# k and q of both head halves ahead of v in a segment-recurrent attention kernel

## The chip, the cores and the metric

One core of one Trainium2 chip. The metric is the device time of one execution in microseconds (us), the median of several. In the profiles PE is the tensor engine, DVE the vector engine, ACT the scalar engine, POOL GpSimd, SP the engine whose queue asks for the weights.

## The reference, cut to what matters

```python
for s in range(64):                       # 2048 tokens in segments of 32
    h = concat([mem, x[32*s:32*s+32]])    # 8 + 32 = 40 rows of 1024
    q, k, v = h @ Wq, h @ Wk, h @ Wv      # 32 heads of 128 each
    p = softmax(where(mask, q @ k.T * scale, -1e9))
    o = (p @ v) @ Wo
    mem = o[:8]                           # the next segment needs this
    outs.append(o[8:])
# then: g * a + (1 - g) * b with b = gelu(x @ w_gate) * (x @ w_up) @ w_down
```

The 64 segments form a chain through mem. Everything else (the feed-forward branch b) has no such chain.

## The kernel before

Each segment is done in two halves of 16 heads (r = 0, 1). The weights of q, k, v and o come in 64 pieces of 512 KB (matrix, half, eighth). They don't all fit into the on-chip memory, so 12 slots are shared by the same eighth of the two halves: after the piece of half 0 has been used, the slot is fetched again for half 1. The next segment takes the halves in the other order, so that one fetch per shared slot and segment is enough.

```python
PAIRS = {"k": (0, 2), "q": (0,), "v": (0, 1, 2, 3, 4, 6), "o": (0, 2, 4)}   # eighths that share a slot
def seq(m, r):        # shared pieces first in half 0, last in half 1
    ...
    return p + f if r == 0 else f + p
walk = both(0) + one("v", 0) + both(1) + one("o", 0) + one("v", 1) + one("o", 1)   # both = k and q
...
def spent(k):         # after the last use of piece k
    n = home[k]
    done[n] += 1
    if done[n] < len(uses[n]) and uses[n][done[n]] != k:
        fetch(n)      # SP asks for the other half's piece
```

Work is hung into this walk of 64 projection steps with `on(matrix, half, step, function)`. "Evac" copies a finished projection out of PSUM, the memory that PE writes; "turning" is transposing by PE; "scores" is q times k, "attend" is the softmax result times v; a_bf is the output of a segment in bf16. The parts that matter:

```python
on("v", 0, 0, lambda: evac(bank_of["k", 0], tok))     # PSUM -> SBUF
on("v", 0, 0, lambda: evac(bank_of["q", 0], tok2))
on("v", 0, 4, lambda: trans(kT, tok))                 # 4 PE transposes, copy to kT
on("v", 0, 7, lambda: trans(qT, tok2))
on("k", 1, 0, lambda: evac(bank_of["v", 0], vA))
on("k", 1, 2, lambda: scores(0))                      # then softmax on DVE and ACT
...
on("o", 0, 0, some(f1, 4))                            # fill: 4 groups of other matmuls
on("o", 0, 0, lambda: trans(kT, tok))
on("o", 0, 0, lambda: attend(ua))
...
on("o", 0, 1, lambda: scores(1, ...))
# end of a segment: PSUM -> a_bf on ACT, two 128-column transposes of a_bf, two DVE copies
# into hT (the mem rows of the next segment); the store of a_bf waits until on("k", 0, 4)
```

"Fills" f1 and f2 are matmuls for the x rows of later segments. In two of every four segments they produce rows of k and q, which are then stored to qk_scr. Every store belongs to a semaphore lane; a transfer in a lane is issued only when the one before it in that lane has landed.

Of the kernel before, what the change touches and what calls it, by code (L numbers as in the profile page):

```python
# [195 lines left out]
def bass_gated_mix__memory_aug_recurrent_mem_tr__geglu_ffn__prompt_kernel(  # L196
# [35 lines left out]
    with ExitStack() as es:  # L232
# [58 lines left out]
        qT = al("qT", [128, 4, 4, 32])  # L291
        cur[0] += 128
# [6 lines left out]
        vA = al("vA", [128, 4, 128], at=oT.off)  # L299
        tok2 = al("tok2", [128, 512], at=oT.off + 1024)  # L300
        tA = al("tA", [128, 8, 32], at=qT.off)
        tB = al("tB", [128, 8, 32], at=qT.off + 512)
        E8 = al("E8", [128, 8, LQ], at=qT.off + 512)
# [14 lines left out]
        PAIRS = {"k": (0, 2), "q": (0,), "v": (0, 1, 2, 3, 4, 6), "o": (0, 2, 4)}  # L318
# [8 lines left out]
        walk = both(0) + one("v", 0) + both(1) + one("o", 0) + one("v", 1) + one("o", 1)  # L327
# [226 lines left out]
        inits = [k for k in [at_step(p, 0) for p in range(24)] + [(m, 1, i) for m in "kqv" for i in range(8)]  # L554
# [129 lines left out]
        def evac(bank, t):  # L684
            act_copy(t[:, :], PB[bank][:, :], [BK(bank)], [t.r()])

        def trans4(e, t=tok, head=False):
            for j in range(4):
                to = PBV[TT][:, 0:512].rearrange("p (g j y) -> p j g y", g=4, j=4)[:, j] if head else PBV[TT][:, j * 128:(j + 1) * 128]
                ins = e.transpose(to, t[:, j * 128:(j + 1) * 128], ident[:, :])  # L690
            return ins

        def trans_pe(t):
            op("pe", lambda e: trans4(e, t), rd=[t.r(), ident.r()], wr=[BK(TT)])

        def trans(to, t):
            if t:
                trans_pe(t)
            i_ap = PBV[TT][:, 0:512].rearrange("p (j g c) -> p (j g) c", g=4, c=32)
            dve_copy(to[:, :, :, 0:32].rearrange("p j g c -> p (j g) c"), i_ap, [BK(TT)], [to.r()])  # L700
# [5 lines left out]
        def scores(r, mid=None):  # L706
# [18 lines left out]
            op("dve", lambda e: e.tensor_tensor(out=sS, in0=sS, in1=b8(nm, LQ), op=ALU.add), rd=[BK(SS), st8.r(0, 8)], wr=[BK(SS)])  # L725
            op("act", lambda e: e.activation(E8[:, :, :].rearrange("p a c -> p (a c)"), PB[SS][:, 0:320], ACTF.Exp, scale=scale),  # L726
               rd=[BK(SS)], wr=[E8.r()])
            if mid:
                mid()
# [14 lines left out]
        bo = (B0, B1, B2, SS)  # L744

        def attend(u):

            def f(e):
                for j in range(4):
                    for g in range(4):  # L750
                        r = slice(32 * g, 32 * g + 32)
                        ins = e.matmul(PB[bo[g]][:, j * OW:(j + 1) * OW], lhsT=vA[r, j, :],
                                       rhs=tA[r, 2 * j:2 * j + 2, :].rearrange("p a c -> p (a c)"),
                                       start=(j == 0), stop=False, skip_group_check=True)
                return ins
            op("pe", f, rd=[vA.r(), tA.r()], wr=[BK(b) for b in bo])

        def attend_tail(u):
# [9 lines left out]
            for g in range(4):  # L768
                cp[("act", "dve")[g % 2]](oT[:, g, :, :].rearrange("p j c -> p (j c)"), PB[bo[g]][:, 0:n], [BK(bo[g])],
                                          [oT.r(g * n, (g + 1) * n)])  # L770
# [5 lines left out]
        bank_of = {("k", 0): B0, ("q", 0): B1, ("v", 0): B2, ("k", 1): B0, ("q", 1): F2, ("v", 1): B0}  # L776
# [37 lines left out]
        def fill(m, u, b, h=hR):  # L814
            ks = [(m, u, i) for i in range(8) if i not in PAIRS[m]] + [(m, u, i) for i in PAIRS[m]]
            out = []
            for n, k in enumerate(ks):
# [7 lines left out]
                out.append(lambda f=f, w=w: op("pe", f, rd=[h.r(), w.r()], wr=[BK(b)]))  # L825
# [23 lines left out]
        def fill_evac(m, u, b, st):  # L849
            t = st if m == "v" else tok  # L850
            act_copy(t[:, :], PB[b][:, :], [BK(b)], [t.r()])

        def fill_trans(m):
            op("pe", lambda e: trans4(e, tok, m == "q"), rd=[tok.r(), ident.r()], wr=[BK(TT)])

        def fill_put(st, how):
            cp[how](st[:, :].rearrange("p (i x c) -> p x i c", i=4, x=16), PBV[TT][:, 0:512].rearrange("p (x i c) -> p x i c", x=16, i=4),
                    [BK(TT)], [st.r()])
# [36 lines left out]
        for s in range(NSEG):  # L895
# [23 lines left out]
            on("k", 0, 4, some(pend))  # L919
            if s == 0:  # L920
# [15 lines left out]
                on("v", 0, 4, lambda: rest_k(0))  # L936

                def fills_1():
# [4 lines left out]
                    act_copy(tok[:, :], PB[F2][:, :], [BK(F2)], [tok.r()])  # L943
                    mm0("v", 1, F1, st1[1])
                    tr0("q", 1, tok, st1[2])
                on("k", 1, 0, fills_1)
                if NG > 1:
                    on("k", 1, 0, lambda: op("dve", lambda e: e.tensor_copy(hR[:, :, :], hR1[:, :, :]), rd=[hR1.r()], wr=[hR.r()]))
                on("k", 1, 0, lambda: (load_v(0, slice(1, 2)), more_late(99)))
                on("q", 1, 0, lambda: load_h(1))  # L950
            if s > 0:
                on("k", 0, 6, lambda: rest_k(0))
            on("v", 0, 0, lambda: evac(bank_of["k", 0], tok))
            on("v", 0, 0, lambda: evac(bank_of["q", 0], tok2))
            on("v", 0, 4, lambda: trans(kT, tok))
            on("v", 0, 7, lambda: trans(qT, tok2))
            on("k", 1, 0, lambda: evac(bank_of["v", 0], vA))
            on("k", 1, 2, lambda: scores(0))
            on("k", 1, 4, lambda: rest_k(1))

# [4 lines left out]
            on("o", 0, 0, lambda: evac(bank_of["k", 1], tok))  # L965
            on("o", 0, 0, lambda: evac(bank_of["q", 1], tok2))
            on("o", 0, 0, some(f1, 4))
            on("o", 0, 0, lambda: trans(kT, tok))
            on("o", 0, 0, some(f1, 2))
            on("o", 0, 0, lambda: trans_pe(tok2))  # L970
            on("o", 0, 0, lambda: attend(ua))
            on("o", 0, 0, lambda: attend_tail(ua))
            on("o", 0, 0, lambda: trans(qT, None))
            on("o", 0, 0, some(f1))
            if k1:
                on("o", 0, 1, lambda: fill_evac(*k1, F1, stage))
            if uw == 1:
                on("o", 0, 1, lambda: act_copy(part[:, :], PB[F1][:, 0:256], [BK(F1)], [part.r()]))
            on("o", 0, 1, lambda: scores(1, add_part if uw == 0 else None))
            if k1:  # L980
                on("o", 0, 6, lambda: fill_trans(k1[0]))
                on("o", 0, 6, lambda: fill_put(stage, "act"))
                on("o", 0, 6, lambda: fill_store(*k1, G, stage))
            if uw == 0:
                on("o", 0, 6, lambda: store_tail(Q, asum))
            on("o", 1, 0, lambda: evac(bank_of["v", 1], vA))
            on("o", 1, 0, some(f2, 6))
            on("o", 1, 0, lambda: attend(ub))
            on("o", 1, 0, lambda: attend_tail(ub))
            on("o", 1, 0, some(f2))  # L990
            if s % 4 == 0 and Q >= 0:
                on("o", 1, 0, lambda: load_oR(Q, 1))
            if s % 4 == 1 and Q >= 0:
                on("o", 1, 0, lambda: load_oR(Q, 0))
            if not last:
                on("o", 1, 0, lambda: load_qk(s + 1, 0))
                on("o", 1, 0, lambda: load_qk(s + 1, 1))
                on("o", 1, 0, lambda: load_v(s + 1))
                if s + 2 < NSEG:
                    on("o", 1, 0, lambda: load_h(s + 2))  # L1000
            if s % 4 == 2 and G + 1 < NG:
                on("o", 1, 0, lambda: load_r(G + 1))
            if k2:
                on("o", 1, 1, lambda: fill_evac(*k2, F2, stage))
                if k2[0] == "v":
                    on("o", 1, 3, lambda: fill_store(*k2, G, stage))
# [4 lines left out]
            on("o", 1, 2, o_store)  # L1011
# [6 lines left out]
            for t in range(2):  # L1018
                cs = slice(128 * t, 128 * t + 128)
                act_copy(a_bf[:, cs], PB[XO][:, cs], [BK(XO)], [a_bf.r(cs.start, cs.stop)])  # L1020
            if k2 and k2[0] == "q":
                fill_trans("q")
            if not last:
                for t, bk in enumerate((B1, B2)):
                    op("pe", lambda e, t=t, bk=bk: e.transpose(PBV[bk][:, 0:128], a_bf[:, 128 * t:128 * t + 128], ident[:, :]),
                       rd=[a_bf.r(128 * t, 128 * t + 128), ident.r()], wr=[BK(bk)])
                    op("dve", lambda e, t=t, bk=bk, h=h_next: e.tensor_copy(
                        h[:, :, NR:32].rearrange("p (g t) c -> p t g c", t=2)[:, t],
                        PBV[bk][:, 0:128].rearrange("p (g c) -> p g c", g=4)[:, :, NR:32]),
                       rd=[BK(bk)], wr=[h_next.r(32 * kc, 32 * kc + 32) for kc in range(t, KC, 2)])  # L1030
            if k2 and k2[0] == "q":
                fill_put(stage, "dve")

            def store(s=s, k2=k2, G=G):
                op("pool", lambda e: e.dma_start(a_scr[s].rearrange("r (g c) -> g r c", g=4), a_bf[:, :]), rd=[a_bf.r()],
                   wr=[("D", "a", s)], lane="st")
                if k2 and k2[0] == "q":
                    fill_store(*k2, G, stage)
            pend.append(store)
        for f in pend:  # L1040
            f()
# [138 lines left out]
```

## Time and profile before

| | before |
|---|---|
| median of 3 runs | 2208.19 us (2202.38 to 2211.07) |
| span of the profiled run | 2213.4 us, granted PE clock 0.988 |
| head, to the first a_bf | 143.9 us |
| 63 segments, first to last a_bf | 1527.0 us, 24.2 each |
| after the last a_bf (feed-forward) | 542.5 us |

The reading that turned out to matter is when SP asks for the weights. This is its queue in the segment that starts at 658.03 us (start us, us, then the issues):

```profile
658.47 0.34 SPq L378 DMA_DIRECT2D sl<-in_A_Wk_dram  x1
...
661.93 3.08 SPq L378 DMA_DIRECT2D sl<-in_A_Wv_dram  x6
672.36 1.90 SPq L378 DMA_DIRECT2D sl<-in_A_Wo_dram  x3
```

### The profile page before, as it was taken

The page shows a single profiled execution, that of the slowest core. Times are in us where ns is not written, and L with a number is a line of the kernel's source. Part 1 is how long each engine was busy: PE and PEld are TensorE (multiplying, and loading weights), DVE is VectorE, ACT ScalarE, POOL GpSimd, SP SyncE. Part 2 cuts the span into 40 slices and gives each one's busy share as a digit, 9 for nine tenths or more (in the row PEclk, how much of TensorE's full clock was granted, in tenths as well). Part 3 has the DMA queues.
Part 4 walks back from the last instruction along what each step waited for, and adds up shares of the span by engine and source line. Part 5 has one row for each costly group of instructions (what it writes and reads, how often), then busy time and mean ns, then how long its engine had stood idle before and what let it go on. Part 6 is the DMA issues. An engine that isn't in the chain of part 4 may idle for free.

```text
span 2213.4 us, 76738 instructions
## 1 busy us (share of the span) xinstructions
PE 2034.4 (92%) x37840; PEld 934.4 (42%) x32178; DVE 931.1 (42%) x2154; ACT 606.9 (27%) x1296; POOL 625.2 (28%) x1155
## 2 busy tenths in 40 slices
PE   7789998999999999999989999999888999999999
PEld 4334444444444444444444444444344424343343
DVE  6433343334334434434433344344344516254362
ACT  4322222223222232323322232222222303122130
POOL 7223333432433343243334324333321000000000
PEclk9989999999999999999999999999999999999999
DMA  9978887788888888878887888888789400001000
GB/s 366 389 254 277 297 298 271 270 295 303 281 277 314 297 277 304 310 270 299 304 277 271 287 301 289 275 306 297 274 297 371 150 22 29 30 25 34 20 29 20
DMA packets 202660, 528.84 MB, mean 239 GB/s; under 512 B 29592, under 2 KB 46616, under 8 KB 202336
## 3 DMA queue, kind: packets, MB, share of 16 engines
q1 hardware_dynamic: 171760, 466.69, 59.2%
q0 software_dynamic: 30432, 56.99, 8.0%
q8 instruction: 274, 4.49, 0.8%
q10 hardware_dynamic: 144, 0.26, 0.1%
q14 instruction: 50, 0.41, 0.1%
HBM read 490.16 MB, written 33.55 MB: 237 GB/s over the span
## 4 chain that ended last, share of the span: by engine, by line
PE 60%; DMA 23%; POOL 6%; DVE 6%; issue 3%; ACT 1%; SPq 0%; DVEq 0%; POOLq 0%
PE pb L462 16%; PE pb L796 11%; PE pb L779 8%; PE pb L807 7%; DMA a_scr<-a_bf 7%; DMA sl<-in_A_Wk_dram 6%; PE pb L822 5%; DMA sl<-in_A_Wv_dram 4%; PE pb L1135 4%; PE pb L690 3%; DMA sl<-in_A_Wo_dram 3%; POOL v_scr L863 2%; DVE oT L680 2%; DMA xr_scr<-xr 2%; PE pb L837 1%
## 5 line engine op out<-in xcount | busy, mean ns | idle before, releaser
L796 PE MATMUL pb<-sl,hT 128*32 128x512 bf16 x8192 | 665.0, 381 | 48.6 <-issue 22.0
L779 PE MATMUL pb<-sl,hT 128*32 128x512 bf16 x4096 | 398.0, 379 | 0.0
L796 PEld LDWEIGHTS pb<-sl,hT 128*32 128x32 bf16 x8192 | 210.5, 96 | 429.7 <-issue 274.5
L807 PE MATMUL pb<-sl,oT 128*32 128x256 bf16 x8192 | 282.4, 281 | 19.2 <-issue 11.6
L773 POOL COPY oRc<-oT 128x128 bf16<-128x128 bf16 x128 | 96.1, 750 | 654.3 <-DVE oT L680 648.6
L677 ACT ACTIVATE tok<-pb 128x512 bf16<-128x512 f32 x318 | 176.3, 596 | 346.1 <-PE pb L796 320.6
L807 PEld LDWEIGHTS pb<-sl,oT 128*32 128x32 bf16 x8192 | 206.2, 99 | 83.8 <-ACT oT L677 45.2
L822 PE MATMUL pb<-sl,hR 128*32 128x512 bf16 x3072 | 209.9, 384 | 0.0
L462 PE MATMUL pb<-xT,wg 128*128 128x512 bf16 x768 | 182.8, 381 | 5.0 <-DMA wg<-in_B_w_gate_dram 5.0
L680 DVE COPY kT<-pb 128x512 bf16<-128x512 bf16 x128 | 53.2, 416 | 319.0 <-PE pb L690 287.4
L462 PE MATMUL pb<-xT,wu 128*128 128x512 bf16 x768 | 181.8, 380 | 0.0
L680 DVE CAST oT<-pb 128x256 bf16<-128x256 f32 x256 | 96.7, 419 | 182.9 <-PE pb L762 182.9
L690 PE MATMUL pb<-ident,tok 128*128 128x128 bf16 x1272 | 126.6, 222 | 48.9 <-DVE kT L680 42.6
L1135 PE MATMUL pb<-wd,GT 128*32 128x512 bf16 x1568 | 152.2, 379 | 0.0
L779 PE MATMUL pb<-wd,GT 128*32 128x512 bf16 x1568 | 152.2, 379 | 0.0
L677 ACT ACTIVATE vA<-pb 128x512 bf16<-128x512 f32 x128 | 76.4, 597 | 270.5 <-PE pb L796 270.5
L450 ACT ACTIVATE s<-pb 128x512 f32<-128x512 f32 x112 | 66.9, 597 | 291.5 <-PE pb L462 291.5
L690 PEld LDWEIGHTS pb<-ident,tok 128*128 128x128 bf16 x1272 | 72.0, 98 | 158.8 <-DVE kT L680 90.8
L677 ACT ACTIVATE oT<-pb 128x256 bf16<-128x256 f32 x256 | 84.3, 381 | 189.9 <-PE pb L762 189.9
L451 DVE SCALAR_TENSOR_TENSOR tp<-s,pb 128x512 f32<-128x512 f32 x112 | 76.7, 685 | 125.9 <-ACT s L450 125.5
L726 ACT ACTIVATE E<-pb 128x320 bf16<-128x320 f32 x128 | 56.0, 438 | 220.5 <-DVE pb L725 220.5
L462 PEld LDWEIGHTS pb<-xT,wg 128*128 128x128 bf16 x768 | 75.0, 98 | 97.5 <-issue 8.7
(104 smaller groups left out, 2230.3 us busy)
## 6 DMA issues: line engine op xcount, KB each, us to landing
sl<-in_A_Wv_dram SPq DMA_DIRECT2D x394, 512.0 KB, 9.3
sl<-in_A_Wo_dram SPq DMA_DIRECT2D x205, 512.0 KB, 5.9
sl<-in_A_Wk_dram SPq DMA_DIRECT2D x142, 512.0 KB, 7.3
sl<-in_A_Wq_dram SPq DMA_DIRECT2D x79, 512.0 KB, 6.6
qkr<-qk_scr POOLq DMA_DIRECT2D x126, 64.0 KB, 2.2
qk_scr<-stg POOLq DMA_DIRECT2D x59, 128.0 KB, 6.2
wd<-in_B_w_down_dram SPq DMA_DIRECT2D x7, 1024.0 KB, 14.8
xq_scr<-xTp SPq DMA_DIRECT2D x4, 1024.0 KB, 17.3
```

The costliest lines, as they stand in the source:

```text
L450: op("act", lambda e: e.activation(s1[:, :], hg, ACTF.Square, scale=SQ), rd=[BK(bg)], wr=[s1.r()])
L451: op("dve", lambda e: e.scalar_tensor_tensor(out=t[:, :], in0=s1[:, :], scalar=1.0, in1=hg, op0=ALU.add, op1=ALU.mult), rd=[BK(bg), s1.r() ...
L462: ins = e.matmul(PB[bk][:, 0:FB], lhsT=w[:, kc, cc:cc + 128], rhs=x[:, :, :, kc, :].rearrange("p t i c -> p (t i) c"), start=(kc == 0), st ...
L677: op("act", lambda e: e.activation(o, i, ACTF.Copy), rd=rd, wr=wr)
L680: op("dve", lambda e: e.tensor_copy(o, i), rd=rd, wr=wr)
L690: ins = e.transpose(to, t[:, j * 128:(j + 1) * 128], ident[:, :])
L773: op("pool", lambda e: e.tensor_copy(oRc[:, u, :, :].rearrange("p c (g j) -> p g j c", g=4), diag), rd=[oT.r()], wr=[oRc.r(128 * u, 128 * ...
L779: return e.add_instruction(mybir.InstMatmult(name=nc.get_next_instruction_name(), start_tensor_calc=start, stop_tensor_calc=stop, tile_siz ...
L796: ins = again(e, g, *at, one, end) if k[0] == "q" else e.matmul(*at, start=one, stop=end)
L807: ins = e.matmul(PB[XO][32 * g:32 * g + 32, 0:256], lhsT=oT[:, gp_, 2 * jj + hh, 0:32], rhs=w[:, c:c + 256], start=(r == 0 and one and hh ...
L822: ins = e.matmul(PB[b][32 * g:32 * g + 32, :], lhsT=h[:, k[2], :], rhs=w[:, g * 512:(g + 1) * 512], start=(n == 0), stop=(n == 7))
L1135: ins = again(e, q, *a, j == 0, j == NJ - 1) if hf else e.matmul(*a, start=(j == 0), stop=(j == NJ - 1))
```

## The change

The intent: bring the scores of both halves early, so that no attend waits for a softmax, and take PE's small waits out (turning k and q, a_bf at the end of a segment). fq is a new staging tile for the q rows of a fill; an "excursion" is a break in the projections for transposes. Core of the diff; banks, the fills of the first segment and helper functions are cut.

```diff
-        vA = al("vA", [128, 4, 128], at=oT.off)
+        vA = al("vA", [128, 4, 128], at=tok.off)
+        qT = al("qT", [128, 4, 4, 32], at=oT.off)
+        fq = al("fq", [128, 512], at=oT.off)
-        PAIRS = {"k": (0, 2), "q": (0,), "v": (0, 1, 2, 3, 4, 6), "o": (0, 2, 4)}
+        PAIRS = {"k": (0, 2), "q": (0, 2), "v": (0, 1, 2, 3), "o": (0, 1, 2, 3)}
-        walk = both(0) + one("v", 0) + both(1) + one("o", 0) + one("v", 1) + one("o", 1)
+        walk = both(0) + both(1) + one("v", 0) + one("o", 0) + one("v", 1) + one("o", 1)
-        bo = (B0, B1, B2, SS)
+        bos = ((XO, B0, B1, B2), (B0, B1, B2, SS))         # attend of half 0 off the scores' bank
+            def turn():                                    # one excursion of 8 transposes
+                trans8(tok, tok2)
+                heads(kT, "act", 0)
+                heads(qT, "dve", 512)
+            on("k", 1, 2, turn)
+            on("k", 1, 4, lambda: scores(0))
+            on("v", 0, 6, turn)
+            on("o", 0, 0, lambda: halves(bank_of["v", 0]))
+            on("o", 0, 0, some(f1, 1))
+            on("o", 0, 0, lambda: scores(1))
+            on("o", 0, 0, some(f1, 1))
+            on("o", 0, 0, lambda: attend(ua, 0))
             # end of a segment
-                act_copy(a_bf[:, cs], PB[XO][:, cs], ...)
+                cp[eng](a_bf[:, cs], PB[XO][:, cs], ...)   # half on ACT, half on DVE
+            run(f2)                                        # rest of the fill covers a_bf
-                    e.transpose(PBV[bk][:, 0:128], a_bf[:, 128 * t:128 * t + 128], ident[:, :])
+                    for g in range(4):                     # 32-column tiles
+                        e.matmul(PB[bk][32 * g:32 * g + 32, 0:32], lhsT=a_bf[:, c:c + 32], ...)
             # a k/q fill is now turned and stored at the start of the next segment
+                        trans8(stage, tok, True)
+                        fill_put(stage, "act")
+                        fill_put(fq, "dve", 512)
+                        fill_store(*k1, G, stage)          # both stores: lane "fq"
+                        fill_store(*k2, G, fq)
```

## The prediction

> **What bounds the kernel now.** I first cut the span into stretches, then asked for the period of one segment, then for who keeps the tensor engine (PE) waiting, then for the chain in single segments, and last for the transfers.
>
> The recurrence is 64 segments in series. The copies into a_bf, two per segment, give its period: (1670.9 - 143.9)/63 = 24.2 us. So 63 periods are 1527 of the 2213 us. The change touches little outside them: the head (to 144 us) and the feed-forward stage (from 1671 us) keep their work.
>
> ```profile
> L677 ACT ACTIVATE a_bf<-pb x128: 271/275/278, 143.9 to 1670.9; 128x128 bf16<-128x128 f32 x128
> ```
>
> ```profile
> 400.00:800.00 400.00, 367.37 (x8460) 178.45 (x7428) 164.45 (x446) 118.06 (x271) 143.79 (x274) 1.00 0.83 292
> ```
>
> In the middle of the recurrence PE is busy 92% (367.37 of 400) and the DMA engines 83% at 292 GB/s. Neither is full, and both are near it. The period is PE's work plus waits. The waits, from 160 to 1650 us (each line: us in total, times, longest):
>
> ```profile
> PE pb L690 <- DVE kT L680: 25.7, 25, 2.2
> ...
> PE pb L796 <- issue: 22.0, 18, 1.9
> PE pb L711 <- DVE qT L680: 17.2, 57, 0.3
> ...
> PE pb L796 <- DMA sl<-in_A_Wk_dram: 13.7, 18, 1.5
> PE pb L1025 <- ACT a_bf L677: 13.0, 34, 0.4
> PE pb L807 <- issue: 11.6, 17, 1.5
> ```
>
> L690 is the turning of k and q, L711 the scores, L1025 the turning of the mem rows, L796 the projections. Behind the first line stands a store: pA shares its bytes with a_bf, so softmax waits until a_bf has reached memory, and kT queues behind it on DVE. The chain shows it, and shows the other long link, the weights of k, which land only just in time:
>
> ```profile
> 294.07 6.71 DMA a_scr<-a_bf
> ...
> 300.88 0.44 DVE pA L732
> ```
>
> ```profile
> 609.96 9.19 DMA sl<-in_A_Wk_dram
> ```
>
> So a weight piece asked for at the start of a segment can need 9 us. This is the start and the middle of the segment that begins at 633.9 us (last two numbers: DMA share, GB/s):
>
> ```profile
> 635.90:639.40 3.50, 3.50 (x64) 1.17 (x44) 0.42 (x1) 1.09 (x2) 1.32 (x3) 1.00 0.88 254
> ...
> 643.90:648.90 5.00, 4.70 (x168) 3.61 (x160) 3.48 (x10) 1.92 (x5) 0.95 (x2) 1.00 1.02 414
> ```
>
> The first microseconds of a segment, with the small loads and stores of the POOL queue in flight, move 254 GB/s at nearly full share; later 414. Stores are slow to land:
>
> ```profile
> qk_scr<-stg POOLq DMA_DIRECT2D x59, 128.0 KB, 6.2
> ...
> a_scr<-a_bf POOLq DMA_DIRECT2D x64, 64.0 KB, 7.0
> ```
>
> **What the Trainium skill says.** "DMA: Bandwidth & Descriptors", in "Anatomy of one DMA — SWDGE (gpsimd) path", gives a fixed cost of about 2.0 us plus bytes/436 GB/s, says that the fixed part is mostly the receipt, and that a semaphore wait is done by the issuing sequencer before dispatch. For 128 KB that makes 2.3 us; the fastest store from stg here took 2.7, the median 6.2, so the trace agrees only where the engines are idle. "Perfetto Trace Analysis", in "Tensor Engine Instruction (MATMUL, LD_WEIGHTS)", says that ACT, DVE and GpSimd are strict FIFO; the pA-then-kT link above is that. "TensorEngine Tiling (Array Packing)", in "Key Properties", says that a switch of tiling mode drains the array; the trace of before fits: four transposes take 0.33 us between projections while their starts are 56 ns apart (0.22 us).
>
> **The change part by part.** (1) k and q of both head halves come first, then v. The two turns of one half become one excursion of eight transposes: about 8 x 0.056 + 0.1 = 0.55 against 2 x 0.33 us, so -0.1 us each, twice a segment: -0.2. (2) Attend for half 0 writes other banks than the scores, so the scores of half 1 go ahead of attend and no longer wait for qT: the eight o-matmuls ahead of them take 0.70 us from start to the scores where 0.33 would do, -0.35. (3) Softmax of half 0 is ready long before its attend, so the kT wait goes: 25.7/62 = -0.4. (4) At the end ACT and DVE evacuate a_bf side by side and four groups of fill matmuls (4 x 0.216 = 0.86 us) run meanwhile, which hides the a_bf wait of some 0.45: -0.45. (5) The mem rows are turned by small 32-column matmuls and copied by two engines: -0.1. Sum: -1.5 us a segment, 63 x 1.5 = -95 us, if nothing takes its place. The unnamed "issue" stalls (33.6 us in all) stay.
>
> Two things take its place.
>
> (6) **The window of the k and q weights.** A shared slot is refetched after its use in half 0 and needed at the end of half 1. Before, v of half 0 lay in between, and three pieces had about 9.5 us. Now four pieces have: 28 groups x 0.216 = 6.0, plus turn and scores 0.9, plus start 0.2, about 7.1 us for the first and 7.8 for the last. Three pieces landed 9 to 10.5 us after the segment's start in the segments that I looked at, for the reason in the two stretches above. By 10 us about four pieces' worth of bytes had moved, so I put the fourth at 9 to 10.5, and the wait at 1.2 to 2.7 us. After that the v pieces (4) and o pieces (4) follow; eight pieces at 1.28 us each (512 KB at 410 GB/s) plus 3 us to start and 1.5 to end the segment make about 14.4 us from the end of k and q. That gives 23.5 us for a landing at 9, 24.9 at 10.5 and 22.2 if the weights come in time. I take 23.5: -0.6 us against the 24.1 of such segments.
>
> (7) **A new store on qT's memory.** The order of instructions of the changed kernel shows what the diff only hints at: fq, the staging tile of the precomputed q rows, and qT lie on the same bytes. In the segments after a k/q fill, DVE copies fq, POOL stores stg and then fq, and qT is written only when the second store has landed:
>
> ```
> POOL  DMACopy qk_scr<-stg 128x4x128 [waits a_act_2]
> POOL  DMACopy qk_scr<-fq 128x4x128 [waits a_dve_3,a_fq_49]
> DVE   TensorCopy qT<-pb 128x512 [waits a_fq_49,a_act_2]
> ```
>
> Both stores are in one lane, so the second is issued only after the first has landed. This stands in 29 of the 64 segments. The times: trans at 1.4 to 2.0 us after the start, copy to stg until 2.6, store 1 issued at 2.7, landed after 6.2 (the median; it shares the queue with the weights) at about 9; store 2 issued by 9.8, landed 2.7 later (the engines are idle by then) at 12.5; qT 0.4, scores 0.35, at 13.2; the last 8 groups of k and q 1.7: done at 15. Without it this point comes at 7.8 to 10.5. From there at least 13 us of PE work follow: 28 us. Had store 1 taken 4 us and store 2 3 us, it would be 25.5. PE stands at the scores for 5 to 7 us while DVE, strictly in order, holds qT. I take 28.0 against 24.4: +3.6.
>
> Sum: 34 x (-0.6) + 29 x 3.6 = -20 + 104 = +84 us. From 2208 that makes about 2290; I say 2285.
>
> **The rivals.** (a) The plain gain: no new wait binds; -95 us and up to -2.4 us a segment where the k weights no longer bind, 2060 to 2115. For it: every part removes a measured wait, and the work looks tuned. Against: the listed waits of qT on the store are in the program, and no store of 128 KB landed in under 2.7 us, so two in series from 2.7 us cannot be done before 2.7 + 2.7 + 0.8 + 2.7 = 8.9, some 3 us after the scores want qT. (b) Gain and loss cancel: the stores land fast (9 to 10.5), which is when the weights land anyway, so both waits are one; FQ segments at 25, others at 22.5 to 23.5: 2130 to 2220. For it: waits that overlap do not add. (c) The DMA chain binds everywhere: after each wait the v fetches start late and o is late too, 25 in all segments and 28 to 29.5 in the 29: 2340 to 2400. For it: the DMA share of 0.83 leaves little slack and each pause of the queue is lost.
>
> **Range and chances.** The middle is between (b) and (c). Range 2130 to 2400. Faster by over 2% (under 2164) needs fast stores and weights in time: 0.2. Within 2%: 0.2. Slower: 0.6.
>
> **What would show it.** Right if in the profile after: DVE's qT waits for DMA qk_scr<-fq (or POOL's second store for the first) 29 times by several us; PE at the scores (L713) waits for qT by over 100 us in total; the a_bf and kT waits of PE are nearly gone; the periods alternate, two long and two short in every four; PE waits for Wk or Wq grow from 13.7 us. Wrong if PE does not idle at L713, or if all four kinds of segment have one length. I would be too high if the stores land in 3 us each, too low if the v and o fetches arrive late as well.

## More of the kernel before

From the page of the profile of before: the span in 40 slices (granted PE clock and DMA share, in tenths), then the chain that ended last.

```profile
PEclk9989999999999999999999999999999999999999
DMA  9978887788888888878887888888789400001000
...
PE 60%; DMA 23%; POOL 6%; DVE 6%; issue 3%; ACT 1%; SPq 0%; DVEq 0%; POOLq 0%
```

The recurrence is slices 4 to 30: clock at nine tenths or more in all of them, DMA engines around 0.8.

## The result, and the profile after

Ratios here and below are the mean time of one kernel's fast runs over that of the other's of the same rounds, so not quite the ratio of the medians quoted.

| | before | after |
|---|---|---|
| median | 2208.22 us (4 runs) | 2709.23 us (2699.9 to 2714.55, 4 runs) |
| ratio | 1 | 1.227, 95% interval 1.222 to 1.231 |
| span of the profiled run | 2213.4 us | 2703.4 us |
| head, to the first a_bf | 143.9 us | 151.0 us |
| 63 segments | 1527.0 us | 2010.1 us |
| after the last a_bf | 542.5 us | 542.3 us |

Slower was right; 2285 was far too low, and so was the top of the range, 2400. All but 7 us of the loss lies in the 63 segments. The copies into a_bf (first, last) and the same middle stretch of the recurrence in the kernel after:

```profile
L677 ACT ACTIVATE a_bf<-pb x64: 277/278/278, 151.0 to 2161.1; 128x128 bf16<-128x128 f32 x64
```

```profile
400.00:800.00 400.00, 296.47 (x6336) 139.94 (x5568) 129.03 (x338) 91.11 (x214) 110.67 (x209) 0.90 0.66 218
```

PE is busy 296 of 400 us (367 before), the granted clock fell to 0.90 from 1.00, and the DMA engines move 218 GB/s where they moved 292. Everything idles more. The page of after says the same over the whole span:

```profile
PEclk9888899888989898989898999999898999999999
DMA  9856666666666675767676666766667791000000
...
PE 50%; DMA 40%; issue 3%; DVE 3%; ACT 2%; SPq 1%; POOL 0%; POOLq 0%; DVEq 0%; ACTq 0%
```

The chain that ended last is 40% DMA, not 23%. The segments have two lengths. By segment number modulo 4, from the start of one segment's projections to the next: 34.7, 34.6, 28.7 and 29.8 us (before 24.6, 24.2, 24.4, 23.8). The long ones are those that turn and store a k/q fill. There are 29 of them; two of the first two groups, segments 60 and 61, do not. The 29 alone take 35.1 us (24.4 before), all others 29.2 (24.1 before). The waits after, from 160 to 2140 us:

```profile
PE pb L713 <- DVE qT L680: 231.9, 122, 8.1
DVE qT L680 <- DMA qk_scr<-fq: 230.7, 29, 9.3
...
POOL qk_scr L870 <- DMA qk_scr<-stg: 191.2, 29, 7.9
...
PE pb L801 <- DMA sl<-in_A_Wv_dram: 69.6, 56, 2.6
...
PE pb L812 <- DMA sl<-in_A_Wo_dram: 50.2, 63, 1.7
...
PE pb L784 <- DMA sl<-in_A_Wq_dram: 40.3, 37, 2.9
```

The first three lines are the store that the prediction named: PE stands at the scores (L713) because qT waits for the store of fq, whose issue waits for the store of stg, 29 times. The last three are late weights, each of them small or absent before. The kT wait of PE is gone from the list, and PE at the turning of the mem rows (now L1036) waits for a_bf 2.1 us in the whole run, where it was 13.0.

The chain of one long segment, which starts at 763.70 us (start us, us, what):

```profile
766.88 7.62 DMA qk_scr<-stg
...
774.98 2.39 DMA qk_scr<-fq
...
777.46 0.43 DVE qT L680
...
789.42 8.76 DMA sl<-in_A_Wo_dram
```

So two stores one after the other, and later a second hold-up by an o piece. What the stop does to PE is in the instructions around it (start us, busy us, line; the bracket is idle time before):

```profile
770.01 0.39 PE L784 MATMUL pb<-sl,hT 128*32 128x512 bf16 x4
777.94 0.46 PE L713 MATMUL pb<-mS,ident 128*32 128x320 bf16 x4 [7.54 <-DVE qT L680]
...
778.87 0.64 PE L784 MATMUL pb<-sl,hT 128*32 128x512 bf16 x4
779.30 0.64 PE L801 MATMUL pb<-sl,hT 128*32 128x512 bf16 x4
```

and in two stretches of the same segment (the third number from the end is the granted clock):

```profile
766.70:770.20 3.50, 3.50 (x68) 1.09 (x32) 0.82 (x2) 0.60 (x1) 0.79 (x1) 1.00 0.94 249
...
777.20:780.70 3.50, 2.76 (x48) 0.86 (x40) 1.87 (x4) 0.44 (x1) 0.29 (x1) 0.50 0.00 0
```

After 7.5 us of idleness PE works at half its clock: groups of four matmuls start 0.43 us apart, which before the stop took 0.22. The Trainium skill, "TensorE: Matmul & The Clock Gate", in "Part 1: The HAM clock gate (the "warmup" mystery)", says that the array falls to half its clock after an idle window of about 3.4 us and needs about as long of sustained work to come back; this trace agrees on the fall, with 0.50 granted and 2.76 us of work in that stretch. The return took a little longer here: the granted clock is 0.50 from 773.4 to 783.7 us and 1.00 after that, so PE, which set to work again at 777.94, needed about 5.8 us.

Last, SP's queue in an ordinary segment of after, which starts at 835.04 us and is 27.6 us long, beside that of before shown above:

```profile
835.49 0.34 SPq L378 DMA_DIRECT2D sl<-in_A_Wk_dram  x1
...
845.57 1.96 SPq L378 DMA_DIRECT2D sl<-in_A_Wv_dram  x4
850.37 2.11 SPq L378 DMA_DIRECT2D sl<-in_A_Wo_dram  x4
```

```profile
844.04:847.04 3.00, 2.19 (x40) 1.05 (x32) 1.42 (x4) 1.20 (x2) 0.22 (x1) 1.00 0.18 42
```

The v pieces are asked for 10.5 us after the start, not 3.9. By then nothing is left on the queue: around that moment (the last line is the stretch from 9 to 12 us) the DMA engines move 42 GB/s. Over segments 5 to 58, the ordinary ones of after and all of before, the mean figures from the traces are these:

| us | before | after, ordinary |
|---|---|---|
| from the start to the request for v | 3.9 | 11.8 |
| from there to the last packet of weights | 17.9 (9 pieces, and the rest of k and q) | 15.2 (8 pieces) |
| from there to the end of the segment | 2.5 | 2.3 |

In both kernels the segment ends soon after its last weights. The request for v comes 7.9 us later, and the shorter stream after it gives back 2.8: that is the loss of some 5.1 us in each of these segments.

### The profile page after: what moved, and what is told of

Read it like the earlier page. It is cut to its first block, busy times and chain, and to the rows that moved or that the text cites. A ratio compares the mean times of both kernels' runs of the same rounds, so it can differ in the third digit from the quotient of the medians.

```text
span 2703.4 us, 77876 instructions
## 1 busy us (share of the span) xinstructions
PE 2129.1 (79%) x38218; PEld 965.3 (36%) x32556; DVE 979.6 (36%) x2220; ACT 628.4 (23%) x1359; POOL 628.1 (23%) x1155
## 4 chain that ended last, share of the span: by engine, by line
PE 50%; DMA 40%; issue 3%; DVE 3%; ACT 2%; SPq 1%; POOL 0%; POOLq 0%; DVEq 0%; ACTq 0%
PE pb L462 13%; DMA sl<-in_A_Wo_dram 12%; DMA sl<-in_A_Wq_dram 11%; PE pb L801 9%; DMA qk_scr<-stg 8%; PE pb L784 7%; PE pb L812 6%; PE pb L827 4%; DMA sl<-in_A_Wv_dram 4%; PE pb L1157 3%; DMA qk_scr<-fq 3%; PE pb L691 2%; PE pb L846 2%; DVE qT L680 1%; ACT kT L677 1%
## 5 line engine op out<-in xcount | busy, mean ns | idle before, releaser
L801 PE MATMUL pb<-sl,hT 128*32 128x512 bf16 x8192 | 733.5, 412 | 145.9 <-DMA sl<-in_A_Wv_dram 70.5
L784 PE MATMUL pb<-sl,hT 128*32 128x512 bf16 x4096 | 429.9, 410 | 41.5 <-DMA sl<-in_A_Wq_dram 41.4
L801 PEld LDWEIGHTS pb<-sl,hT 128*32 128x32 bf16 x8192 | 227.3, 102 | 625.6 <-issue 343.7
L827 PE MATMUL pb<-sl,hR 128*32 128x512 bf16 x3072 | 228.8, 408 | 10.3 <-DMA sl<-in_A_Wk_dram 4.9
L713 PE MATMUL pb<-mS,ident 128*32 128x320 bf16 x512 | 45.4, 345 | 233.2 <-DVE qT L680 232.5
L680 DVE COPY qT<-pb 128x512 bf16<-128x512 bf16 x128 | 54.3, 424 | 461.2 <-DMA qk_scr<-fq 230.7
L677 ACT ACTIVATE tok<-pb 128x512 bf16<-128x512 f32 x225 | 130.8, 596 | 287.5 <-PE pb L801 236.7
L677 ACT ACTIVATE kT<-pb 128x512 bf16<-128x512 bf16 x128 | 76.4, 597 | 342.7 <-POOL kT L890 218.4
L680 DVE CAST vA<-pb 128x256 bf16<-128x256 f32 x128 | 54.3, 424 | 227.1 <-ACT vA L677 227.1
L677 ACT ACTIVATE vA<-pb 128x256 bf16<-128x256 f32 x128 | 49.2, 384 | 348.8 <-PE pb L801 348.7
L713 PEld LDWEIGHTS pb<-mS,ident 128*32 128x32 bf16 x512 | 13.4, 95 | 303.0 <-DVE qT L680 301.0
```

What stands on the lines that cost most here:

```text
L677: op("act", lambda e: e.activation(o, i, ACTF.Copy), rd=rd, wr=wr)
L680: op("dve", lambda e: e.tensor_copy(o, i), rd=rd, wr=wr)
L713: e.matmul(PB[SS][q, 0:320].rearrange("p (a c) -> p a c", a=4), lhsT=ident[:, q], rhs=mS[:, :].unsqueeze(1).to_broadcast([128, 4, 80]), st ...
L784: return e.add_instruction(mybir.InstMatmult(name=nc.get_next_instruction_name(), start_tensor_calc=start, stop_tensor_calc=stop, tile_siz ...
L801: ins = again(e, g, *at, one, end) if k[0] == "q" else e.matmul(*at, start=one, stop=end)
L827: ins = e.matmul(PB[b][32 * g:32 * g + 32, :], lhsT=h[:, k[2], :], rhs=w[:, g * 512:(g + 1) * 512], start=(n == 0), stop=(n == 7))
```

## The experiments

Theory A, formed from this: there are two losses. The weights, which came in one long stream, now come in two bursts (k and q, then v, then o right behind), each asked for when the matrix before is done and each awaited by itself; that costs some 5.2 us (5.1 by the count above) in all 63 segments. On top of it, the two stores stop 29 segments. The rivals are named with each run. In all, 15 kernels ran.

### Taking the store stop out: fq_apart, fq_mem, fq_lane

```diff
-        fq = al("fq", [128, 512], at=oT.off)
+        fq = al("fq", [128, 512], at=part.off)         # fq_apart, fq_mem: bytes idle in these segments
-                   ... wr=[("D", "qk", G, m4)], lane="fq")
+                   ... wr=[("D", "qk", G, m4)], lane=f"f{m}")   # fq_apart, fq_lane: a lane each for k and q
```

> The change, with fq on bytes that are idle then and each qk_scr store in a semaphore lane of its own, so that neither qT nor the second store waits for the first. Theory A (two losses, one on top of the other: 29 segments that stop for the qk_scr stores, worth 5.6 us each beyond the others, and all 63 paying 5.2 us for weight fetches that now come in bursts): 2709 - 29 x 5.6 = about 2545 us, all segments alike at 28.5 to 29.5 us. Rival B (the stop only hides the wait for weights, as the order of fetches binds in those segments too): the time stays above 2650.

> As fq_apart, but both qk_scr stores still in one semaphore lane: only the bytes shared with qT are taken out. If the shared bytes are what stops the segment: 2530 to 2570, as fq_apart. If the lane is (the GpSimd queue stands at the second store until the first has landed, and the load of kT's old rows is behind it): 2650 to 2710, as the change. Something between says that both count.

> The change with each qk_scr store in a semaphore lane of its own and nothing else: fq and qT still share their bytes. qT then waits for the store of fq, which is issued at about 3.7 us and not at 10.7, and lands with the other at about 10 to 10.5. If the serial lane was the main cost: the 29 segments lose about 2.5 us of their 5.6 to 6.2, 2709 - 29 x 2.5 = about 2635, range 2600 to 2670. If lane alone is enough: 2530 to 2560. If the shared bytes hold as before: above 2690.

| | own bytes | own lanes | median us | ratio to before |
|---|---|---|---|---|
| the change | no | no | 2709.2 | 1.227 |
| fq_mem | yes | no | 2686.7 | 1.216 (1.209 to 1.223) |
| fq_lane | no | yes | 2639.3 | 1.197 (1.192 to 1.202). It was run at another time. |
| fq_apart | yes | yes | 2529.5 | 1.146 (1.139 to 1.152) |

The stop costs 180 us, 6.2 a segment in the 29, and all four kinds of segment of fq_apart are now alike (28.6 to 29.5 us), as theory A had it. Neither cause alone is worth 180: bytes alone 22, lanes alone 70. With the lane kept, POOL stands at the second store, its copy of kT's old rows is behind that, qT is behind kT, and PE waits at the scores as before. With the bytes kept, qT still waits for one store; this is inside the 2600 to 2670 expected. PE's wait for qT at the scores in fq_mem, then in fq_lane, and last the five longest waits of PE in fq_apart, each in the whole run:

```profile
PE pb L713 <- DVE qT L680: 215.0, 116, 7.6
```

```profile
PE pb L713 <- DVE qT L680: 183.0, 125, 6.2
```

```profile
PE pb L784 <- DMA sl<-in_A_Wq_dram: 94.8, 69, 3.4
PE pb L801 <- DMA sl<-in_A_Wv_dram: 60.7, 53, 2.4
PE pb L812 <- DMA sl<-in_A_Wo_dram: 58.9, 77, 1.9
PE pb L801 <- DMA sl<-in_A_Wk_dram: 43.2, 49, 2.3
PE pb L713 <- DVE qT L680: 37.4, 119, 3.4
```

What stands at the top in fq_apart are weights of all four matrices, 257.6 us together. This is the second loss alone.

### No repeated fetches: fq_nofetch, before_nofetch

```diff
-            if done[n] < len(uses[n]) and uses[n][done[n]] != k:
+            if done[n] < len(uses[n]) and uses[n][done[n]] != k and not (paired(uses[n][done[n]]) and paired(k)):
```

This is wrong on purpose: one half computes with the other's pieces. These two runs, and the two of the next part, still passed the comparison with the reference. I take it that the attention outputs are too small beside the feed-forward ones for its tolerance (the reference scales Wq to Wo by 0.05 and by the root of their width), but did not test that. They are measurements, not kernels to use.

> fq_apart without the repeated fetches: after the first segment the 12 shared slots are not filled again, so every segment computes with stale weights (a wrong result on purpose) and the PE work is the same. It shows what the new order costs when weights never make it wait. Theory A (late weights cost the rest): the 4.1 us a segment that PE waited for weights in fq_apart go, so 2530 - 63 x 4.1 = about 2270, and less if the TensorE clock recovers; close to before_nofetch. Rival E (the order of the PE work itself is longer, through stops for qT and vA and a lower clock): above 2350.

> The kernel before, with the repeated fetches left out in the same way (wrong on purpose). PE waited for weights 0.4 us a segment there, plus 0.5 us put down to issue: 2150 to 2190. If more than 3% comes off, the kernel before was bound by its fetches more than its waits showed.

Measured: fq_nofetch 2095.1 us (0.948, 0.946 to 0.951), before_nofetch 2096.4 us (0.948, 0.945 to 0.951). Both below what I expected. So the fetches cost 112 us in the kernel before, where the waits named 'weights' add up to a fifth of that, and 2529.5 - 2095.1 = 434 us in the new order. Without them the two kernels are the same to 0.1%: **while no weights are late, the order and all the parts that should gain are worth nothing in the end**. The busy time of before_nofetch, of fq_nofetch and of fq_apart:

```profile
PE 2004.1 (96%) x37842; PEld 924.5 (44%) x32178; DVE 933.0 (45%) x2154; ACT 606.8 (29%) x1296; POOL 624.1 (30%) x1155
```

```profile
PE 1952.4 (93%) x38220; PEld 944.1 (45%) x32556; DVE 979.0 (47%) x2220; ACT 625.0 (30%) x1359; POOL 627.0 (30%) x1155
```

```profile
PE 2103.8 (83%) x38220; PEld 964.5 (38%) x32556; DVE 980.6 (39%) x2220; ACT 631.7 (25%) x1359; POOL 627.1 (25%) x1155
```

The third against the second: the same number of PE instructions is busy 151 us longer, at a granted clock of 0.954 against 0.995. So about a third of the 434 us is slower work, and the rest (281 us) is idle PE; that is why the waits for weights in fq_apart sum to 257.6 us only.

Between the first two, PE is busy 52 us less. Its waits, of before_nofetch and of fq_nofetch (160 to 1530 us), say where they went:

```profile
PE pb L711 <- DVE qT L680: 18.4, 61, 0.3
PE pb L1025 <- ACT a_bf L677: 12.7, 33, 0.4
```

```profile
PE pb L713 <- DVE qT L680: 54.2, 122, 1.9
PE pb L755 <- DVE vA L680: 19.8, 60, 0.9
PE pb L801 <- DVE hT L680: 18.2, 58, 0.3
```

The a_bf wait went (12.7 to 1.1) and a wait for hT came (18.2), in the same place: the filled gap ended, and then nothing was left to run while the mem rows were copied. The one excursion leaves the scores right behind the turn, so PE waits for qT (54.2 against 18.4), and vA, evacuated in halves just before attend, is waited for (19.8). All lines of the two lists sum to 40.0 and 96.2 us: 56 us more waiting against 52 us less work.

### One burst at a time: fq_no_kq, fq_no_vo

```diff
-            if done[n] < len(uses[n]) and uses[n][done[n]] != k:
+            if done[n] < len(uses[n]) and uses[n][done[n]] != k and not (k[0] in "kq" and paired(k)):   # or "vo"
```

> fq_apart with the k and q pieces not fetched again (wrong on purpose), the eight v and o pieces kept. fq_apart took 2530, without any repeated fetch 2095: 435 us for twelve pieces. Theory A (two bursts, each with its own start and each awaited by itself): the v/o burst costs about 60% of it, so 2095 + 260 = 2355, range 2280 to 2430, and the sum of the losses of this run and of fq_no_vo is near 435. Rival H (too many bytes for the period, so that bursts disturb each other): a third fewer bytes let nearly all of the loss vanish, under 2200.

> The complement: only the four k and q pieces are fetched again (wrong on purpose). Theory A: the k/q burst alone, landing 10.4 to 11.9 us after the start of a segment where PE wants them at 7 to 8, costs 2.5 to 3.5 us a segment: 2095 + 175 = 2270, range 2230 to 2330. Rival H: four pieces in a segment of 22 us are no load at all: under 2130.

Measured: with the v and o pieces alone 2349.9 us (1.063, 1.060 to 1.066), with the k and q pieces alone 2304.0 us (1.044, 1.040 to 1.049). Over the 2095 without fetches that is 255 and 209, together 464, against 434 for both. Both lie in theory A's ranges, and the losses nearly add. If the sheer number of bytes were the trouble, four pieces in a segment of 22 us would have cost nothing. Theory A holds; a rival of total load falls.

### The split instead of the order: fq_oldpairs, before_newpairs

```diff
-        PAIRS = {"k": (0, 2), "q": (0, 2), "v": (0, 1, 2, 3), "o": (0, 1, 2, 3)}
+        PAIRS = {"k": (0, 2), "q": (0,), "v": (0, 1, 2, 3, 4, 6), "o": (0, 2, 4)}   # fq_oldpairs; before_newpairs the reverse
```

> fq_apart with the paired weights of the kernel before (k 2, q 1, v 6, o 3 pieces of a segment fetched again, against k 2, q 2, v 4, o 4) in the new order. Theory A (order alone): within 2% of fq_apart, about 2500 to 2600. Rival D (the fourth k/q piece, which lands last at 10.4 to 11.9 us, is what binds): a piece less there is 1.3 to 3 us of 63 segments, 2350 to 2460.

> The kernel before with nothing changed but the choice of shared pieces, to the one of the change (k 2, q 2, v 4, o 4 in place of k 2, q 1, v 6, o 3). In the old order k and q have the v projections between their two halves and the burst never pauses. Theory A (the order costs, not the split): 2190 to 2250. Rival D (a fourth k/q piece is late in either order): 2280 or more.

Measured: fq_oldpairs 2618.3 us (1.186, 1.180 to 1.191), 89 more than fq_apart; before_newpairs 2293.5 us (1.037, 1.034 to 1.040), 84 more than before in the same rounds. The first is above the ranges of both theories. The second misses theory A and is what rival D named, a time of 2280 or more, but a late q is the smaller part of it. Each order has its own split, and the other's costs some 85 us in it. In the new order six v pieces have too little time: PE waits 242.1 us for Wv, where fq_apart had 60.7. In the old order, before_newpairs waits for o and for q:

```profile
PE pb L807 <- DMA sl<-in_A_Wo_dram: 72.4, 75, 2.5
PE pb L779 <- DMA sl<-in_A_Wq_dram: 33.3, 43, 1.8
```

So the split was rightly changed with the order: the old split makes the new order still slower, and the new split costs the old order 84 us, not 322.

### The old order with the rest of the change: oldwalk

fq_apart with the old walk and the old split; evacuations, turns, scores and fills re-hung to match it (cut):

```diff
-        walk = both(0) + both(1) + one("v", 0) + one("o", 0) + one("v", 1) + one("o", 1)
+        walk = both(0) + one("v", 0) + both(1) + one("o", 0) + one("v", 1) + one("o", 1)
-                on("v", 0, 6, turn)        # half 1
+                on("o", 0, 0, turn)        # after three fill groups
```

> fq_apart with the projections in the order of the kernel before (v(0) between k(0),q(0) and k(1),q(1)) and its choice of paired weights; the single excursion, the separate attend banks and the 32-column mem turns stay. Theory A (the order of the fetches costs the 5.2 us, the other parts gain the predicted 1.5): 63 x 1.5 = 95 us below before, about 2115, range 2080 to 2180. Rival C (one of the other parts costs too): above 2230; by how much says how much of the loss is not the order's.

Measured: 2287.1 us (1.037, 1.031 to 1.042), 242 below fq_apart and 79 above before; the expected 2115 is missed by far, and rival C's mark, 2230, is passed. The order (with its split) thus returns most of the 322 us between fq_apart and before. fq_oldpairs has the same old split in the new order and took 2618.3, so at one split the order, with what had to be re-hung, is worth 331 us. The largest PE waits that remain are not for weights (the largest of those is 13.8 us, for Wo):

```profile
PE pb L713 <- DVE qT L680: 45.4, 67, 3.7
PE pb L691 <- DVE tok L680: 32.6, 41, 1.6
PE pb L755 <- DVE vA L680: 30.5, 58, 1.0
```

I put them down to how I hung the single turn of half 1 behind o(0), where vA, which lies on tok's bytes, must wait for the turn; no run tested that. It does not show that no good arrangement exists, only that this one gains nothing.

### Two small gains on the kernel before: before_plus

```diff
-            on("k", 0, 4, some(pend))      # store of a_bf
+            on("k", 0, 0, some(pend))
             # and the change's end of a segment: a_bf on ACT and DVE, 32-column turns, copies on DVE and ACT;
             # without the fill that the change runs between them
```

> The kernel before with two small parts: the store of a_bf issued at the start of the next segment and not after four projections (that takes the wait of softmax, and with it kT, for that store), and the change's end of a segment (a_bf on ACT and DVE side by side, mem rows turned in 32-column tiles). If these two waits are worth what the list of waits says (kT 0.43 us, a_bf 0.23 a segment): 2208 - 63 x 0.6 = 2170. If, as in the change, waits for hT and for weights take their place: 2200 to 2215.

Measured in 5 rounds: 2208.1 us, ratio 0.999 (0.997 to 1.001). The same, as the second forecast had it, but not for its reason: the edit hardly removed what it was meant to. Softmax still waits 30.0 us for the store (34.0 before), PE 18.0 us for kT (25.7) and 12.5 for a_bf (13.0). So the run does not show what these waits are worth.

### Why a burst is slow: fq_2k, before_2k, fq_keep, before_keep

In the bursts looked at, the first 4 us move about 190 to 270 GB/s, later 360 to 410. Windows of fq_apart from 2 to 20 us of the segment that starts at 761.08:

```profile
763.08:767.08 4.00, 4.00 (x72) 1.15 (x36) 0.97 (x2) 1.19 (x2) 1.53 (x4) 1.00 0.84 262
767.08:770.08 3.00, 1.98 (x52) 0.55 (x36) 1.83 (x5) 0.44 (x1) 0.29 (x1) 1.00 0.93 374
770.08:773.08 3.00, 1.77 (x20) 0.68 (x20) 1.42 (x4) 1.19 (x2) 0.22 (x1) 0.80 0.04 14
773.08:777.08 4.00, 3.62 (x68) 1.82 (x64) 0.77 (x2) 0.94 (x2) 0.00 (x0) 0.72 0.84 192
777.08:781.08 4.00, 4.00 (x148) 3.21 (x140) 3.65 (x10) 0.99 (x3) 0.77 (x1) 1.00 1.00 388
```

The small transfers of the POOL queue, which the prediction named beside the slow start, are not needed for it: from 773 to 777 us, where the v burst moves under 200 GB/s, no packet of that queue is in the trace. Two more guesses were tested: rows of 4 KB, and the pause.

```diff
-            op("sp", lambda e: e.dma_start(dst(t, k), src(k)), wr=[t.r()], lane=lane)
+            for c in (slice(0, 1024), slice(1024, 2048)):      # fq_2k, before_2k: shared k, q, v in halves of the columns
+                op("sp", lambda e, c=c: e.dma_start(t[:, c], src(k)[:, c]), wr=[t.r(c.start, c.stop)], lane=...)
```

```diff
-            if done[n] < len(uses[n]) and uses[n][done[n]] != k:
+            if done[n] < len(uses[n]) and (uses[n][done[n]] != k or paired(k) and k[0] == "k"):   # fq_keep
             # before_keep: k[0] == "v" and k[2] in (4, 6)
```

> fq_apart with each k, q and v piece fetched as two DMAs of half the columns, so that every row of a transfer is 2 KB and not 4 KB. After each pause the 4 KB rows moved at only 230 to 270 GB/s for some 4 us. Theory F (it is the 4 KB rows that start slowly; o pieces of 2 KB rows did not once): the pieces land 1.5 to 2 us earlier in both bursts, 2530 - 63 x 3 = about 2340, range 2280 to 2420. Rival G (any burst starts slowly after a pause): 2500 to 2570.

> The kernel before with the same split into 2 KB rows. Theory F: its one slow start a segment goes, the waits for Wk (0.22 us a segment) with it: 2180 to 2205, and first packets of a segment at 150 to 170 ns for 4 KB instead of 250. Rival G: 2200 to 2230.

> fq_apart plus useless traffic: after its use in the second half each of the two shared k pieces, which are right for the next segment as they stand, is fetched once more into its own slot. That is 1 MB more a segment, put into the pause between the k/q burst and the v burst. Theory K (a pause is what makes the next burst start at 250 GB/s): the v pieces, now behind two others in a running stream, still land earlier than 16.9 to 22.7, at about 15.5 to 19.5; 2 to 3 us a segment, 2340 to 2420. Rival L (every burst is slow in its first 4 us or pieces, pause or not, or the rate is set by something else at that time): the duplicates only stand in the way, 2540 to 2650.

> The kernel before plus two duplicate v fetches (1 MB a segment) behind the last o piece, to fill the pause from 21 us to 2 us of the next segment. Theory K: the k and q pieces land at 4 to 7 us in place of 5 to 9.2 and the waits for them go, 2150 to 2195. Rival L: 2210 to 2260, more traffic and nothing won.

Measured: fq_2k 2578.2 us (1.167, 1.164 to 1.170), before_2k 2226.3 us (1.008, 1.005 to 1.011). Smaller rows made both slower (the second by under 1%), so it is not the rows. fq_keep 2571.9 us (1.166, 1.159 to 1.173), 42 above fq_apart and in rival L's range. The duplicates filled most of the pause, with a DMA share of 0.72 ahead of the v burst where fq_apart has 0.04, and the v burst was slow all the same; from 12 us on in the segment of fq_keep that starts at 774.80 (from 9 to 12 us it moved 228 GB/s):

```profile
786.80:790.80 4.00, 3.62 (x128) 2.81 (x132) 2.52 (x7) 1.93 (x5) 0.04 (x1) 1.00 0.81 237
790.80:794.80 4.00, 2.72 (x72) 1.60 (x60) 1.91 (x6) 0.00 (x0) 0.73 (x1) 1.00 0.99 360
```

before_keep took 2393.3 us (1.086, 1.081 to 1.091), but that run is spoilt: the fills of two segments in four read the very slots that the duplicates rewrite, and PE waits there.

```profile
PE pb L822 <- DMA sl<-in_A_Wv_dram: 142.1, 60, 5.9
```

Its other two kinds of segment take 23.5 and 24.6 us, against 23.8 and 24.6 before: nothing won there either. Both guesses fall, as far as a pause that is not quite filled can say. What makes the first pieces of a burst slow stays open; that it happens once more per segment in the new order is shown.

## Why the prediction was wrong

The direction was right, and both hold-ups that the prediction named are there. Their sizes were not right, and for the ordinary segments not even the sign: they were to gain 0.6 us. Slower was forecast for the sake of part 7 alone; fq_apart, without its stop, is still 15% slower. By the prediction's own steps:

**Parts 1 to 5, "-1.5 us a segment", -95 us.** This failed. Without fetches the two kernels differ by 1.4 us in all. The removed waits are gone, as said, and PE's work is 52 us shorter. But I took the time of each removed wait as a gain and did not ask what PE would wait for one instruction later: hT behind a_bf, qT behind the single turn, vA behind its halves took back 56 us. Part 4 was too large from the start: the list of waits gives 13.0 us over 62 segments for a_bf, 0.2 each and not 0.45.

**Part 6, "I take 23.5", the step that failed most.** Measured 29.2 us in the ordinary segments: +5.1 against before, not -0.6. The mechanism, late k and q and then v and o behind them, was right; each term of its sum was too small. The fourth k/q piece was to land at 9 to 10.5 us, and the sum took 9; in the ordinary segments of after the last k/q packet comes at 10.7 us, and v is asked for at 11.8. "Eight pieces at 1.28 us each" and "3 us to start" are 13.2 us; measured 15.2. The v burst starts slowly again, and o is asked for only when o(0) uses its own, 5.2 us after v. "1.5 to end the segment" was 2.3. (The three terms are 14.7, and not the 14.4 that the text adds up.) So 2.8 us are the late end of k and q, 2.0 the burst of v and o and 0.8 the end. The runs with one burst each put 209 us on k and q and 255 on v and o. The old order had hidden both under the v projections: asked for at 3.9 us, v followed k and q without a break. I had seen both facts, the slow first microseconds and the continuous stream in the middle, and put the landing at the early end of my own range.

**Part 7, "+3.6" in 29 segments.** The mechanism was exact: 29 waits, two stores in one lane, qT behind them, and it takes both the bytes and the lane. In size it was too small. Beyond what happens to the ordinary segments I had 3.6 + 0.6 = 4.2 us; measured, the long ones lost 10.7 and the ordinary ones 5.1, so 5.6 apart, and removing the stop gave 6.2. In the segment at 763.70 the stores landed at 10.8 and 13.7 us after the start (I had 9 and 12.5). So the last 8 groups of k and q began at 14.7 and not 13.2, and they took 3.4 us and not 1.7, because PE ran at half its clock after the stop: k and q ended at 18.2, where I had 15. From the scores (projections from 778.45) to the next turn (784.18) the same 14 groups took 5.7 us, where they take 3.1 without fetches, and the chain names no wait in between. I gave the stop its length and nothing for what it does to PE afterwards.

**The sum.** What all segments lost beyond the forecast: 63 x (5.1 + 0.6) = 359 us; the long segments' excess: 29 x (5.6 - 4.2) = 41; the head 7. Together 407, which is the 406 by which the span's +490 exceeds the +84 predicted.

**The rivals.** (c), "The DMA chain binds everywhere", had the right mechanism, and the prediction even says that it would be "too low if the v and o fetches arrive late as well". I put it at 25 us and 28 to 29.5; it is 29.2 and 35.1. The waits for the two bursts nearly add (464 us singly, 434 together), and the clock that falls with them was in no rival. All signs listed for "right" came true (29 waits for the store, over 100 us at the scores, a_bf and kT gone, two long and two short, Wk and Wq up) and that did not make the number right: they test the mechanism, not its size.

## What to carry to other kernels

When an order of work also sets when transfers are asked for, write down for each transfer the moment of its request and the moment of its use, in both kernels, before counting instructions: here twelve pieces a segment cost 112 us in one order and 434 in the other. A wait that is removed is a gain only down to the next operand that is late in the same place; here 52 us of gain came back as 56 us of other waits. And a long stop of PE can cost more than its length: here PE worked for 5.8 us at half its clock after a stop of 7.54 us.

## What the Trainium skill lacked or had wrong

- No page has the slow first microseconds of a burst of weight fetches: about 4 us at 190 to 270 GB/s, then 360 to 410, in the bursts of fq_apart shown above, both with 4 KB rows. It was so with most of the pause filled too (fq_keep: 237 GB/s behind a DMA share of 0.72). Its cause is open.
- "DMA: Bandwidth & Descriptors", in "Anatomy of one DMA — SWDGE (gpsimd) path", gives 2.0 us plus bytes over 436 GB/s for a store from GpSimd. The 128 KB stores of stg took a median of 2.4 us in before_nofetch, which agrees, and 6.2 with the weights on the engines. The section has no figure for such a store beside bulk loads, here 2.6 times as long.
